# Attention outputs turned by the DMA crossbar instead of TensorE, and operand splits queued behind the division of the values, in a fused routing-attention and feed-forward kernel

## Chip, cores, metric

The kernel runs on one core of one Trainium2 chip. The metric is device microseconds of one execution; lower is better. A run is called slow when it lies over 1.5% above the fastest run of the same kernel, and slow runs are left out of all comparisons. Names: PE is TensorE, PEld its weight loads, DVE is VectorE, ACT is ScalarE, POOL is GpSimd, SP is SyncE. L378 is line 378 of the kernel.

## The reference

Clustered attention for 4 batches and 8 heads (768 rows of 64), then a feed-forward with h·cos(h) on all 3072 tokens:

```python
def _attn_ref(q, k, v, centroids):
    ...                                   # q_n, k_n, c_n: rows divided by their norms
    q_assign = np.argmax(np.einsum('bhsd,hcd->bhsc', q_n, c_n), axis=-1)
    k_assign = np.argmax(np.einsum('bhsd,hcd->bhsc', k_n, c_n), axis=-1)
    mask = q_assign[:, :, :, None] == k_assign[:, :, None, :]
    scores = np.where(mask, scale * np.matmul(q, k.transpose(0, 1, 3, 2)), -1e9)
    ...                                   # softmax
    return np.matmul(attn, v).astype(np.float32)

def _moe_ref(x, w_in, w_out):             # x: (3072, 512), d_ff 2048
    h = x @ w_in
    return ((h * np.cos(h)) @ w_out).astype(np.float32)
```

## The kernel before

Heads go in 16 pairs, four to a batch. A pair passes through these steps. `split` (DVE, half of it on POOL or ACT for some pairs) makes high and low fp16 parts of q and k. `tr`/`tr_out` or `tr_dma` turn them. `c_mm`/`c_post` find the clusters. `e_chunk` makes nine chunks of scores on PE (L332) with one exponential each on ACT (L339). `f_mm` multiplies by the values (L352) and `norm` divides (L362, L363). `g_tr` turns the result into `xt`, the feed-forward's input. After each fourth pair the feed-forward of that batch runs (`moe1`, L394 on PE, L401 on ACT, L402 on DVE; `moe2`, L416).

The turn of a pair's output, and what it waits for:

```python
    def norm(p, hh):
        av = f_of[p, hh]
        ...
        nc.vector.reciprocal(recip, av[:, :, D:DE])                         # L362
        dve_mark[0] = nc.vector.tensor_tensor(                              # L363
            out=av_of[p][:, :, hh, :], in0=av[:, :, 0:D],
            in1=recip.to_broadcast([P, NT, D]), op=ALU.mult).ins

    def g_tr(p):
        b, hp = divmod(p, HPB)                                              # HPB = 4
        ...
        if p >= NPE and hp < HPB - 1:                                       # NPE = 5
            nc.sync.dma_start_transpose(out=xt_of[b][:, hp]..., in_=st...)  # L373
            return
        trx = ps_one.tile([P, NT, P], FP16, name="one")
        for t in range(NT):                                                 # NT = 6
            nc.tensor.transpose(out=trx[:, t, :], in_=st[:, t], identity=ident)   # L378
        dve_mark[0] = nc.vector.tensor_copy(out=xt_of[b][:, hp, :], in_=trx...).ins  # L379
```

The first phase (pairs 0 to 4) is ordered by hand on all engines; its end, before the change:

```python
        for n_f, n_x in ((2, 0), (2, 1), (2, 1), (2, 1), (0, 0)):
            for _ in range(n_f):
                fl.pop(0)()            # value products of pair 3
            for _ in range(n_x):
                ex.pop(0)()            # g_tr of pairs 0, 1, 2
            if not n_x:
                sp.pop(0)()            # a split of pair 5
            chunk()                    # scores and exponential
        g_tr(s - 1)                    # pair 3
```

From pair 5 on ACT and POOL are ordered by hand, and a scheduler orders PE, DVE and SP from the order in which work is given. For pair s, r = s % 4, the work beside the nine chunks was given as

```python
            fill += trs("E", s)        # splits of a later pair: pair 9 in s = 8, pair 13 in s = 12
            if r != 1:
                fill += f_list(s - 1) + g_list(s - 1)   # values, division, turn of the pair before
```

The loads of q and k of pairs 9 and 13 are issued by POOL in the stretch before that of pairs 8 and 12, that is beside the scores of pairs 7 and 11, at chunks 3 (q) and 5 (k).

The softmax here doesn't subtract the row's maximum and nothing guards it: scores larger than these inputs give would overflow.

## Time and profile before

| | kernel before |
|---|---|
| time, median of 3 runs | 315.12 us (314.93 to 315.14) |
| span of the profiled run, granted clock | 313.0 us, 1.0 |
| PE busy / weight loads | 97% / 68% |
| ACT, DVE, POOL busy | 69%, 60%, 24% |
| turns of outputs on PE (L378), copies (L379) | 48 matmuls, 8 copies |
| turns of outputs by the crossbar (L373) | 8 |

Busy time of PE is modelled and matmuls overlap, so 97% says that PE is rarely without work, not that every instruction on it counts. What counts is which wait ends last in a stretch.

### The profile page before, as it was taken

Reading aid. Unit: us, or ns where it says so; the run is one execution under the profiler, and the core shown is the slowest. Engines: PE = TensorE matmul, PEld = TensorE weight load, DVE = VectorE, ACT = ScalarE, POOL = GpSimd, SP = SyncE. Lnnn points to the kernel's source line nnn. Section 1 sums busy time; section 2 is a strip of 40 time slices with the busy share of each in tenths; the row PEclk is TensorE's granted clock in tenths of the full one; section 3 lists DMA queues with packets and bytes.
Section 4 is the critical chain, followed back from the end, with each engine's and each line's share of the span. In section 5 each row is a group of like instructions: output and inputs, shape, how many; then the busy total and the mean of one; then the engine's idle time right before and its main releaser. Section 6 shows DMA issues by size and latency. Waiting matters only on the chain.

```text
span 313.0 us, 8197 instructions
## 1 busy us (share of the span) xinstructions
PE 303.1 (97%) x3459; PEld 213.8 (68%) x3459; DVE 189.0 (60%) x363; ACT 216.4 (69%) x235; POOL 74.7 (24%) x130
## 2 busy tenths in 40 slices
PE   7999999999999999899999999899999999999995
PEld 3668777888765766588775657497865657767754
DVE  5888897779966335369967144458965114455431
ACT  6688988955569999656659999756559996442220
POOL 2979945120130322210040233211020220000000
PEclk9999999999999999999999999999999999999999
DMA  6669999766596989837498997927576472000012
GB/s 213 203 141 185 218 113 146 168 153 153 78 241 131 154 128 150 163 104 172 70 229 127 177 114 180 162 86 179 87 165 99 80 74 61 12 24 36 34 57 80
DMA packets 87845, 40.25 MB, mean 129 GB/s; under 512 B 76352, under 2 KB 82752, under 8 KB 87808
## 3 DMA queue, kind: packets, MB, share of 16 engines
q1 hardware_dynamic: 57504, 24.19, 33.5%
q0 software_dynamic: 30016, 15.21, 33.1%
q8 instruction: 27, 0.44, 0.6%
q10 hardware_dynamic: 288, 0.33, 0.4%
q14 instruction: 10, 0.08, 0.1%
HBM read 27.30 MB, written 6.29 MB: 107 GB/s over the span
## 4 chain that ended last, share of the span: by engine, by line
PE 84%; DVE 7%; DMA 4%; ACT 1%; issue 1%; SPq 0%; POOL 0%; POOLq 0%; ACTq 0%; DVEq 0%
PE big L394 25%; PE one L416 24%; PE big L332 17%; PE one L352 8%; DMA qk_nat<-in_k_dram 4%; PE one L250 2%; PE one L247 2%; PE one L306 2%; DVE g L402 2%; DVE stg L200 2%; PE one L218 1%; DVE av_stage L363 1%; PE one L433 1%; DMA cn_raw<-in_centroids_dram 1%; PE one L378 1%
## 5 line engine op out<-in xcount | busy, mean ns | idle before, releaser
L339 ACT ACTIVATE e_ring<-big 128x1024 f16<-128x1024 f32 x144 | 138.4, 1030 | 16.1 <-PE big L332 14.8
L401 ACT ACTIVATE cos_t<-big,bias_pi 128x1024 f16<-128x1024 f32 x48 | 53.4, 1112 | 65.5 <-PE big L394 64.2
L416 PE MATMUL one<-w_out_sb,g 128*128 128x512 f16 x368 | 95.7, 379 | 0.0
L394 PE MATMUL big<-xt,w_in_sb 128*128 128x256 f16 x768 | 91.3, 273 | 1.0 <-DVE g L402 0.9
L332 PE MATMUL big<-qkT 128*128 128x512 f16 (+1 forms) x384 | 85.6, 325 | 0.5 <-ACT e_ring L339 0.4
L394 PEld LDWEIGHTS <-w_in_sb 128*128 128x128 f16 x768 | 74.0, 98 | 16.2 <-DVE g L402 1.7
L402 DVE TENSOR_TENSOR g<-big,cos_t 128x1024 f16<-128x1024 f32 x48 | 58.6, 1222 | 38.8 <-ACT cos_t L401 38.8
L416 PEld LDWEIGHTS <-g 128*128 128x128 f16 x368 | 35.0, 98 | 28.0
L332 PEld LDWEIGHTS <-qkT 128*128 128x128 f16 x384 | 32.8, 97 | 25.9 <-issue 4.3
L352 PEld LDWEIGHTS <-e_ring 128*128 128x128 f16 x1152 | 43.1, 97 | 7.0
L352 PE MATMUL one<-v_ext,e_ring 128*128 128x65 f16 x1152 | 45.2, 193 | 0.0
L421 DVE COPY o_sb<-one 128x512 f32<-128x512 f32 x23 | 15.8, 687 | 43.3 <-PE one L416 43.3
L200 DVE SCALAR_TENSOR_TENSOR stg<-qk_nat,stg 128x384 f16<-128x384 f32 x64 | 33.3, 553 | 0.2
L134 POOL DMA_DIRECT2D v_ext<-in_v_dram x32 | 26.5, 833 | 4.8 <-issue 2.4
L117 POOL COPY pace<-e_ring 1x1 f16<-1x1 f16 x30 | 5.7, 189 | 79.0 <-ACT e_ring L339 78.8
L117 POOL COPY pace<-g 1x1 f16<-1x1 f16 x13 | 2.3, 177 | 78.9 <-DVE g L402 70.1
L196 POOL TENSOR_SCALAR stg<-qk_nat 128x384 f16<-128x384 f32 x16 | 19.3, 1205 | 6.8 <-DMA qk_nat<-in_q_dram 5.7
L363 DVE TENSOR_TENSOR av_stage<-one,recip 128x384 f16<-128x384 f32 x32 | 17.7, 557 | 1.0
L362 DVE RECIPROCAL recip<-one 128x6 f32<-128x6 f32 x32 | 6.1, 192 | 19.4 <-PE one L352 19.4
L194 ACT ACTIVATE stg<-qk_nat 128x384 f16<-128x384 f32 x28 | 13.1, 512 | 1.9 <-DMA qk_nat<-in_q_dram 1.9
L318 DVE TENSOR_SCALAR qkT<-one 16x768 f16<-16x768 f16 (+1 forms) x20 | 10.9, 544 | 3.5 <-PE one L306 2.9
L258 DVE TENSOR_REDUCE csum<-one 128x192 f32<-128x384 f32 x22 | 11.2, 549 | 0.0
(57 smaller groups left out, 163.6 us busy)
## 6 DMA issues: line engine op xcount, KB each, us to landing
out_dram<-o_sb SPq DMA_DIRECT2D x23, 256.0 KB, 2.4
qk_nat<-in_q_dram POOLq DMA_DIRECT2D x10, 384.0 KB, 4.7
qk_nat<-in_k_dram POOLq DMA_DIRECT2D x10, 384.0 KB, 4.6
v_ext<-in_v_dram POOLq DMA_DIRECT2D x32, 96.0 KB, 4.0
w_in_sb<-in_moe_w_in_dram POOLq DMA_DIRECT2D x4, 512.0 KB, 6.3
w_out_sb<-in_moe_w_out_dram POOLq DMA_DIRECT2D x4, 512.0 KB, 6.1
qk_nat<-in_q_dram SPq DMA_DIRECT2D x5, 384.0 KB, 5.2
qk_nat<-in_k_dram SPq DMA_DIRECT2D x5, 384.0 KB, 5.9
```

The lines of the kernel that those rows point to most:

```text
L134: nc.gpsimd.dma_start(out=v_bufs[p % NV][:, hh, :, 0:D], in_=v[b, 2 * hp + hh].rearrange("(p t) d -> p t d", p=P))
L196: nc.gpsimd.tensor_scalar_mul(dst[:, :, 0, :], src, ASCALE)
L200: nc.vector.scalar_tensor_tensor(out=dst[:, :, 1, :], in0=src, scalar=ASCALE, in1=dst[:, :, 0, :], op0=ALU.mult, op1=ALU.subtract)
L332: mm = nc.tensor.matmul(ps[:, x:x + n], lhsT=qkT[p, 1, hh][:, jt * P:(jt + 1) * P], rhs=qkT[p, 0, hh][:, col:col + n], start=True, stop=True)
L339: nc.scalar.activation(out=e_flat[:, base + c * CW:base + (c + 1) * CW], in_=ps, func=AF.Exp, scale=1.0 / SUNIT)
L352: nc.tensor.matmul(av[:, i, :], lhsT=e_ring[:, r + j, i * P:(i + 1) * P], rhs=vx[:, j, 0:DE], start=(j == 0), stop=(j == NT - 1))
L363: dve_mark[0] = nc.vector.tensor_tensor(out=av_of[p][:, :, hh, :], in0=av[:, :, 0:D], in1=recip.to_broadcast([P, NT, D]), op=ALU.mult).ins
L394: mm = nc.tensor.matmul(ps[:, fi, :], lhsT=w_in_sb[:, ft, (f0 + fi) * P:(f0 + fi + 1) * P], rhs=xt_of[b][:, ft, cols], start=(ft == 0), st ...
L401: nc.scalar.activation(out=cos_t, in_=ps, func=AF.Sin, bias=bias_pi2, scale=1.0)
L402: dve_mark[0] = nc.vector.tensor_tensor(out=g[:, f0:f0 + FQ, :], in0=ps, in1=cos_t, op=ALU.mult).ins
L416: nc.tensor.matmul(ops, lhsT=g[:, f, i * P:(i + 1) * P], rhs=w_out_sb[:, f, :], start=(f == 0), stop=(f == NFPT - 1))
L421: nc.vector.tensor_copy(out=o_sb, in_=ops)
```

## The change

The intent is to take turns off PE and to stop a queued split from holding up a division that needs nothing from it. The whole diff:

```diff
@@ g_tr
-        if p >= NPE and hp < HPB - 1:
+        if hp < HPB - 1:
             nc.sync.dma_start_transpose(...)
             return
@@ end of the first phase
-        ex = [lambda p=p: g_tr(p) for p in range(s - 1)]
@@ in each unit of the first phase
             if f:
                 norm(*f)
+                if f[1]:
+                    g_tr(f[0])
@@ last five chunks
-        for n_f, n_x in ((2, 0), (2, 1), (2, 1), (2, 1), (0, 0)):
-            for _ in range(n_f):
-                fl.pop(0)()
-            for _ in range(n_x):
-                ex.pop(0)()
-            if not n_x:
+        for i in range(5):
+            if fl:
+                take(min(2, len(fl)))
+            if i in (0, 4):
                 sp.pop(0)()
             chunk()
@@ work beside the chunks of pair s
-            fill += trs("E", s)
+            if r:
+                fill += trs("E", s)
             if r != 1:
                 fill += f_list(s - 1) + g_list(s - 1)
+            if not r:
+                fill += trs("E", s)
```

## The prediction

> **What bounds the kernel now.** I read the page first, then the chain of waits, then the timeline of single engines in the stretches the diff touches. From the page, the busy line of each engine and the granted clock:
>
> ```profile
> PE 303.1 (97%) x3459; PEld 213.8 (68%) x3459; DVE 189.0 (60%) x363; ACT 216.4 (69%) x235; POOL 74.7 (24%) x130
> ...
> PEclk9999999999999999999999999999999999999999
> ```
>
> TensorE (PE) is covered for 97% of 313.0 us at full clock, so time is won in two ways only: PE instructions taken away where PE is really the pace, or PE gaps closed. A gap shows in the chain that ended last; these are its consecutive pieces near 116 us (start, length, what):
>
> ```profile
> 114.90 1.03 ACT e_ring L339
> 116.53 5.75 DMA qk_nat<-in_k_dram
> 122.73 0.93 DVE stg L200 x2
> 123.66 0.54 DVE stg L198 x2
> 124.20 0.94 DVE stg L200 x2
> 125.27 0.56 DVE av_stage L363
> 125.97 0.57 DVE av_stage L363
> 126.58 0.51 PE one L378 x6
> ```
>
> A load of keys, then the splits of pair 9 made from it on VectorE (DVE), then the division of the attention values of pair 7 (L363), then the turning of pair 7 on PE (L378), which stands in PE's fixed order before more work. Pair 7's values do not need the load: they are only queued behind the splits in DVE's order. The timeline of PE and DVE there (idle time and releaser in brackets):
>
> ```profile
> 122.90 0.71 PE L352 MATMUL one<-v_ext,e_ring 128*128 128x65 f16 x18
> 123.45 0.59 PE L332 MATMUL big<-qkT 128*128 128x512 f16 x2
> 124.24 0.59 PE L332 MATMUL big<-qkT 128*128 128x256 f16 x3 [0.19 <-ACT e_ring L339]
> 124.67 0.38 PE L416 MATMUL one<-w_out_sb,g 128*128 128x512 f16 x1
> 126.58 0.51 PE L378 MATMUL one<-ident,av_stage 128*128 128x128 f16 x6 [1.54 <-DVE av_stage L363]
> 126.93 0.81 PE L416 MATMUL one<-w_out_sb,g 128*128 128x512 f16 x3
> 127.58 0.60 PE L332 MATMUL big<-qkT 128*128 128x512 f16 x3
> ```
>
> The values of pair 7 are summed at about 123.5, PE has its last other work at 124.67, and stands 1.54 us for L378. The same happens 71 us later for pair 11 (196.40 to 197.84, idle 1.06 us). The waits view sums both: "PE one L378 <- DVE av_stage L363: 2.6, 2, 1.5".
>
> The other place is the end of the first phase, 51 to 60 us, where pairs 0 to 3 are turned on PE. From the timelines of ACT, PE and DVE:
>
> ```profile
> 50.97 9.04 ACT L339 ACTIVATE e_ring<-big 128x1024 f16<-128x1024 f32 x9 [0.56 <-PE big L332]
> 58.44 0.50 PE L378 MATMUL one<-ident,av_stage 128*128 128x128 f16 x6
> 59.14 0.49 PE L394 MATMUL big<-xt,w_in_sb 128*128 128x256 f16 x3
> 59.27 0.55 DVE L379 COPY xt<-one 128x768 f16<-128x768 f16 x1
> 59.89 0.27 PE L394 MATMUL big<-xt,w_in_sb 128*128 128x256 f16 x1
> ```
>
> Nine exponentials run on ScalarE (ACT) back to back, 1.004 us each, until 60.01: here ACT is the pace although PE reads as full. The feed-forward part (L394) starts at 59.14 and stops at its fourth matmul until the copy of pair 3's turned output (L379) ends at 59.82.
>
> **What the Trainium skill says.** (1) "VectorE: DVE Perf Modes", section The three transpose paths: a 128x128 turn takes 390 ns on TensorE into PSUM and 1309 ns through the DMA crossbar straight into SBUF, so the crossbar is slower alone but uses neither PE nor DVE. The trace: six turns in a row hold PE about 0.34 us (54.77 to the next group at 55.11), far under 6 x 390 because they are pipelined, plus a copy of 554 ns on DVE; the existing crossbar turns of outputs (L373, x8) hold the sync queue 1.23 us and land after 2.8/3.7/4.7 us (least, median, most). (2) "DMA: Bandwidth & Descriptors", section Issuing engines are not separate DMA queues: all DMAs share 16 engines and interleave. The DMA row of the page is at 9 tenths or near it in the slices before 60 us, so the new transfers meet the weight loads; the older crossbar turns in such company (ohT) took up to 6.7 us. (3) "Perfetto Trace Analysis", section Identifying the Most-Contended Engine: matmul busy time is no measure of how near PE is to its limit. The trace agrees: the 51 to 60 us stretch shows PE busy in full and is paced by ACT.
>
> **Part A, splits of pairs 9 and 13 behind the values.** Nothing is added or removed. In the stretches of pairs 8 and 12 the four splits (8 DVE instructions, about 3.7 us with 356 and 553 ns each) and their wait for the keys come after pair 7's (11's) division and copy. New order for pair 7: values complete at about 123.5, reciprocal 0.20, division 0.56, hence ready near 124.5. PE finishes what stands ahead of L378 at 124.67 + 0.22 (one matmul of 512 columns, by the 0.43 us that two take) = 124.9. So L378 goes at 124.9, then 0.34, then three L416 at 0.65 in sum, and L332 starts at 125.9 in place of 127.58: **1.7 us**. ACT can follow: its ten exponentials end at 126.08, and before it then stood 2.19 us for PE; the two buffers of "big" free at 125.08 and 126.08, before PE asks. For pair 11: 196.40 + 0.22 + 0.34 + 0.65 = 197.6 against 198.83: **1.2 us**. After that the splits run from about 125.5 to 129.3 and the crossbar turn of pair 9 goes out about 4 us later than at 125.16; it lands in 7.1 us (median of L234), about 136.5, and its first reader (L250, pair 9's centroid product) is at 142.56, less the 1.7. It stays hidden. Everything behind is PE-paced, so 2.9 us reach the end.
>
> **Part B, pairs 0 to 2 by the crossbar.** Removed from 51 to 60 us: 18 turns on PE (3 x 0.34 = 1.0 us) and three DVE copies (3 x 0.554 = 1.66 us). They lie in the ACT-paced stretch: the nine exponentials still end at 60.01 and PE waits more for their buffers (free at 54.99, 55.99, 57.0, 58.0), so the 1.0 us of PE time is not won. What is won: L378 of pair 3 still stands behind the last chunk at 58.0 + 0.43, but DVE has no copy of pair 2 at 57.95, so its split is done by about 58.9 and the copy of pair 3 starts when the turns are done, near 59.0, not 59.27. The feed-forward's fourth matmul comes **0.3 us** earlier; the next "big" buffer, free at 60.01, does not stop it. The added transfers are issued near 31, 41 and 51 us, after each pair's second division (30.43, 40.33, 50.11). The last has 59.14 - 50.7 = 8.4 us to land and takes 3 to 7. The queue they wait in also issues pair 5's loads, which go from 27.4 to about 32.3, but are first used at 54.71.
>
> **Part C, pair 4.** The condition also catches pair 4, which the title does not name: 6 turns and a copy leave PE and DVE near 67 us. There PE stops again at 68.98 for L402 (0.38 us idle), whose own path, from L394's end at 66.53 through L401 and L402 to 68.92, has no turn in it. The 0.34 us of PE only lengthen that gap unless the scheduler puts other work into it: **0 to 0.3 us**, I take 0.1.
>
> Sum: 1.7 + 1.2 + 0.3 + 0.1 = 3.3 us. I take off 0.2 for an order by the scheduler a little worse than assumed (PE, DVE and sync order after 60 us are its own): 3.1 us, hence 315.1 - 3.1 = **312.0 us**.
>
> **Rivals.** (1) Every removed PE instruction counts. For it: PE at 97%. 24 turns x 73 ns (row L378 of the groups: 48 matmuls, 4.0 us busy; in the weight-load row 2.9, 61 ns each) are 1.5 to 2.0 us; with part A's 2.9 this makes 310.2 to 310.7. Against it: ACT without a gap from 50.97 to 60.01. (2) The crossbar turn of pair 2 lands late, behind 512 KB weight loads and pair 4's values, and the feed-forward's first matmuls wait for it. For it: the DMA row is at its fullest at 52 to 58 us. Against it: 8.4 us of room, longest seen for this form 4.7 us. At 10 us it costs 1.5 us, so 313.5; a landing at 12 us brings 315. (3) The splits put off come back: pair 9's operand is late, or DVE, now in arrears at 129, is late with the output copies (L421) or the first L402. For it: splits now end only 2 us before the feed-forward starts. Against it: DVE is half idle there (0.48 mean over 112 to 144 us) and the first L402 in the kernel before starts about 2 us after its L394. It would give back 0.5 to 1.5 us: 312.5 to 313.5.
>
> **Range and chances.** Closing the two gaps is read straight from the trace; I hold it 85% sure to bring at least 2 us. Repeats of the kernel before lie within 0.2 us. Rival 1 pulls to 310.5, rivals 2 and 3 to 313.5: 310.8 to 313.6. Two per cent are 6.3 us, more than all idle PE time the change touches plus all PE time it removes (2.6 + 2.0 = 4.6 us), so faster by over 2% has 2%, slower 1%, within 2% 97%.
>
> **What the profile will show.** Part A right: the wait "PE one L378 <- DVE av_stage L363" gone or under 0.5 us; no wait on qk_nat in the chain near 116 and 188 us; the feed-forward of the second and third batch starts about 2.0 and 3.2 us earlier than at 131.03 and 202.29, counting part B. Part B right: ACT still nine in a row to about 60.0, and L394 resumed near 59.6, not 59.89; wrong if PE gains a full microsecond before 62 us, or if L394 waits on xt from a DMA. Part C right: L378 x24 and L379 x4, L373 x12, with a gap before L394 near 68.7 about as wide or wider than 0.38. The prediction fails if the time is over 313.6, most likely by rival 2 or 3, or under 310.8, by rival 1 or by a new order of the scheduler.

## The result, and the profile after

Ratios here are those for the fast runs of both kernels from the same rounds; they are not quite the ratios of the medians quoted.

| | before | after |
|---|---|---|
| runs | 315.12, 314.93, 315.14, 315.63 us | 311.01, 317.58, 311.77, 320.96 us |
| fast runs | 4 of 4 | 2 of 4 (the others at clock 0.995 and 0.989) |
| span of the profiled run | 313.0 us | 309.2 us |
| ratio of the fast runs | | 0.9879, 95% interval 0.9851 to 0.9907 |

The fast runs gained 3.8 us. Later, with six fast runs, the ratio was 0.9930 (below).

The page of the changed kernel, PE's line and the hardware queue's (packets, MB, share of the 16 DMA engines):

```profile
PE 301.0 (97%) x3435; PEld 212.2 (69%) x3435; DVE 187.6 (61%) x359; ACT 216.3 (70%) x235; POOL 74.9 (24%) x130
...
q1 hardware_dynamic: 60704, 24.98, 39.3%
```

24 matmuls and 4 DVE instructions are gone, which is four pairs, 0, 1, 2 and 4. The hardware queue went from 33.5% to 39.3% of the DMA engines' time.

PE near 124 us in the changed kernel (timeline, columns as in the prediction):

```profile
122.40 0.71 PE L352 MATMUL one<-v_ext,e_ring 128*128 128x65 f16 x18
123.74 0.59 PE L332 MATMUL big<-qkT 128*128 128x256 f16 x3 [0.19 <-ACT e_ring L339]
124.17 0.38 PE L416 MATMUL one<-w_out_sb,g 128*128 128x512 f16 x1
124.39 0.50 PE L378 MATMUL one<-ident,av_stage 128*128 128x128 f16 x6
124.72 0.81 PE L416 MATMUL one<-w_out_sb,g 128*128 128x512 f16 x3
```

L378 follows L416 after 0.22 us, with no idle time. The same holds for pair 11. In the waits view, L378's wait for av_stage is gone.

The end of the first phase in the changed kernel, from the timelines of ACT, PE and DVE:

```profile
51.23 8.45 ACT L339 ACTIVATE e_ring<-big 128x1024 f16<-128x1024 f32 x9 [0.56 <-PE big L332]
58.33 0.50 PE L378 MATMUL one<-ident,av_stage 128*128 128x128 f16 x6
58.82 0.49 PE L394 MATMUL big<-xt,w_in_sb 128*128 128x256 f16 x3
58.87 0.56 DVE L379 COPY xt<-one 128x768 f16<-128x768 f16 x1 [0.15 <-PE one L378]
59.48 1.58 PE L394 MATMUL big<-xt,w_in_sb 128*128 128x256 f16 x13
```

The nine exponentials, which the prediction held to be ACT's own pace, take 8.45 us, not 9.04.

To add up the change I read, from PE's timeline of each profile, the starts of five landmarks: the first score matmul (E0), the first L394 of each of the four feed-forward parts (F1 to F4), and the first matmul of the last output (L433). Differences in us:

| stretch | before | before, second profile | after | after, second profile |
|---|---|---|---|---|
| E0 to F1 | 48.88 | 48.88 | 48.30 | 48.30 |
| F1 to F2 (holds the stretch of pair 8) | 71.89 | 71.40 | 70.00 | 70.72 |
| F2 to F3 (pair 12) | 71.26 | 71.73 | 69.92 | 69.92 |
| F3 to F4 | 62.98 | 62.98 | 62.98 | 62.97 |
| F4 to last | 40.65 | 40.65 | 40.65 | 40.65 |
| sum | 295.66 | 295.64 | 291.85 | 292.56 |

In these four profiles stretches without a wait repeat to 0.01 us, so a stretch shows 0.1 us, which the times of runs do not. Between kernels with different edits they differ by 0.1 to 0.2 us also without a wait (F1 to F2 took 69.80 to 70.11), as the scheduler's order differs. The first profiles differ by 3.81 us: 0.58 before F1, 3.23 in the two stretches with the splits, nothing elsewhere between the landmarks. (Outside them, the start took 10.26 us before and 10.52 after, the end 7.11 and 6.86, which cancels.) Matching PE's instructions one by one, counted from E0, splits the 3.23 (to 0.02): 1.70 and 1.23 us arise at the two L378, 0.09 and 0.10 in the chunks just ahead of them, where the scheduler put the value products in another order, and 0.09 between the first and the fourth L394. The second profile of the changed kernel lost 0.72 us in F1 to F2, where PE stood 0.54 us at 119.66 us for a transfer of one-hot rows (qkT<-ohT).

### The profile page after: what moved, and what is told of

It reads as the page before. It is cut to its first block, busy times and chain, and to the rows that moved or that the text cites. A ratio compares the mean times of both kernels' runs of the same rounds, so it can differ in the third digit from the quotient of the medians.

```text
span 309.2 us, 8154 instructions
## 1 busy us (share of the span) xinstructions
PE 301.0 (97%) x3435; PEld 212.2 (69%) x3435; DVE 187.6 (61%) x359; ACT 216.3 (70%) x235; POOL 74.9 (24%) x130
## 3 DMA queue, kind: packets, MB, share of 16 engines
q1 hardware_dynamic: 60704, 24.98, 39.3%
## 4 chain that ended last, share of the span: by engine, by line
PE 87%; ACT 6%; DVE 4%; DMA 1%; issue 1%; ACTq 0%
PE one L416 25%; PE big L394 25%; PE big L332 18%; PE one L352 9%; ACT e_ring L339 5%; PE one L250 2%; PE one L247 2%; PE one L306 2%; DVE g L402 2%; PE one L218 2%; PE one L433 1%; DMA qk_nat<-in_q_dram 1%; ACT cos_t L401 1%; DVE qkT L318 1%; DVE av_stage L363 1%
## 5 line engine op out<-in xcount | busy, mean ns | idle before, releaser
L416 PE MATMUL one<-w_out_sb,g 128*128 128x512 f16 x368 | 95.7, 379 | 0.0
L394 PE MATMUL big<-xt,w_in_sb 128*128 128x256 f16 x768 | 91.4, 273 | 1.1 <-DVE g L402 1.0
L394 PEld LDWEIGHTS <-w_in_sb 128*128 128x128 f16 x768 | 73.9, 98 | 16.4 <-DVE g L402 2.4
L416 PEld LDWEIGHTS <-g 128*128 128x128 f16 x368 | 35.0, 97 | 28.1
L363 DVE TENSOR_TENSOR av_stage<-one,recip 128x384 f16<-128x384 f32 x32 | 17.8, 557 | 1.1
```

The lines of the kernel that those rows point to most:

```text
L363: dve_mark[0] = nc.vector.tensor_tensor(out=av_of[p][:, :, hh, :], in0=av[:, :, 0:D], in1=recip.to_broadcast([P, NT, D]), op=ALU.mult).ins
L394: mm = nc.tensor.matmul(ps[:, fi, :], lhsT=w_in_sb[:, ft, (f0 + fi) * P:(f0 + fi + 1) * P], rhs=xt_of[b][:, ft, cols], start=(ft == 0), st ...
L416: nc.tensor.matmul(ops, lhsT=g[:, f, i * P:(i + 1) * P], rhs=w_out_sb[:, f, :], start=(f == 0), stop=(f == NFPT - 1))
```

## The experiments

All were run beside the kernel before, on three chips. All gave correct results.

### The changed kernel again

> The changed kernel once more, to have more fast runs and to count slow ones (two of its first four were slow, none of four of the kernel before). Theory: fast runs near 311.4 us, 3.8 us under the kernel before. Rival on the slow state: closing the TensorE gaps makes the clock throttle, then about half of these runs are slow (316 us and more) and the kernel before stays without; if it is a matter of the chip or the moment, few or none are slow here, or the kernel before has some too.

Measured: 311.7 to 313.77 us, median 312.38 (6 runs, all fast); before 314.33 (11 runs); ratio 0.9930 (0.9901 to 0.9958). No run was slow, so the rival's forecast, about half of the runs, failed. Why two of the first four were slow stays open; the kernel before had three runs at clock 0.995 and 316 to 317 us. The gain was smaller than in the first rounds, and the times of the changed kernel spread over 2 us. What follows explains part of the spread.

### Only the new place of the splits

```diff
# to the kernel before: only the last hunk of the change
+            if not r:
+                fill += trs("E", s)
```

> Only the new place of the splits in the stretches of pairs 8 and 12, all turns on TensorE as before. Theory: the two gaps are closed by this alone, 1.80 and 1.33 us by the shift of the feed-forward's starts between the two traces, so about 312.1 us and the wait of L378 for av_stage nearly gone. Rival (the parts need one another, the crossbar turns free DVE and help close the gaps): under 2 us gained.

Measured: 312.72 us median (311.47 to 314.84), ratio 0.9938 (0.9900 to 0.9975). Both gaps before L378 are gone. F1 to F2 took 70.07 us, as in the changed kernel, so this part needs nothing from the others. F2 to F3 took 71.48 us and gained little, because a new wait stood at 142 us, just after F2 (PE and SP timelines of this run):

```profile
142.06 0.77 PE L250 MATMUL one<-cside,qkT 128*128 128x32 f16 x24 [1.39 <-DMA qkT<-stg]
```
```profile
128.78 5.82 SPq L234 DMA_TRANSPOSE qkT<-stg  x1
```

L250 is the centroid product of pair 9. Its operand is the crossbar turn (L234) that goes out after the splits. In the kernel before it went out at 125.16, here at 128.78. The landing times of L234 had least, median and most of 5.5/7.1/7.4 us before and 5.5/7.2/13.2 us here. Without the wait L250 would have started at 140.67, so a transfer with 4.7 us of room by its median became the one that ended last.

This wait (0.3 us or more) was in 5 of the 8 profiles with the new place: this one, and below those with pair 4 on PE (0.35 us), the turns put back (0.61 and 0.39), turn 1 twice (1.77) and turn 1 "later" (0.89). It was in none of the 6 with the old place. The landing itself is later in every profile: the turns of pairs 9 and 13 took 9.7 to 13.6 us in all 8 with the new place, 7.0 to 9.0 us in the 6 with the old one.

### Only the turns by the crossbar

```diff
# to the changed kernel: the last hunk undone
-            if r:
-                fill += trs("E", s)
+            fill += trs("E", s)
...
-            if not r:
-                fill += trs("E", s)
```

> Only the turns of pairs 0, 1, 2 and 4 by the crossbar, the old place of the splits. Theory now: 0.6 us gained, all before 61 us, because three of the nine exponentials at 51 to 60 us were paced by TensorE (starts 1.07 to 1.14 us apart, 0.90 in the changed kernel), so about 314.55 us. The prediction on record said 0.3 to 0.4 us. Rival of every removed instruction counting: 1.5 to 2 us.

Measured: 314.27 us median (312.05 to 315.4), ratio 0.9981 (0.9945 to 1.0017), no sure gain. E0 to F1 took 49.99 us in the profile, 1.11 more than in the kernel before, because of a stop of PE with no releaser (PE timeline of this run):

```profile
50.03 0.40 PE L247 MATMUL one<-cside,qkT 128*128 128x16 f16 x10
52.07 0.50 PE L247 MATMUL one<-cside,qkT 128*128 128x16 f16 x14 [1.64 <-issue]
...
126.76 0.51 PE L378 MATMUL one<-ident,av_stage 128*128 128x128 f16 x6 [0.33 <-DVE av_stage L363]
```

The stop falls within a group of 24 matmuls with the same operands. Less the stop, the stretch took 48.35 us, so 0.53 us of the expected 0.6 was gained and 1.64 lost. The gaps before L378 were here 0.33 and 0.37 us: this stretch came 1.4 us later, and the load of the keys, issued 1.39 us later (117.92 against 116.53), took 4.3 us to land, not 5.8, so that the splits went on at 122.21 against 122.31 us.

### What the stop is

Stops marked "issue" at 50 to 52 us were in 6 of the 10 profiles with early crossbar turns and in none of the 4 without. The DMA packets in the traces (read by start, duration and queue) show what goes with them. I list the start of the 16384-byte fetch on the instruction queue, the longest data packet between 43.5 and 49.5 us, and the stop:

```
profile          early turns   fetch starts   longest data packet    PE stop
before                no         45.52 us       0.97 us                 -
before, second        no         45.56          1.12                    -
only the splits       no         45.28          0.70                    -
early loads           no         45.44          1.07                    -
after                 yes        47.10          0.75                    -
after, second         yes        47.06          0.71                    -
copies put back       yes        47.00          0.88                    -
turn 1 twice          yes        46.70          1.50 (at 47.26)         -
candidate             yes        48.15          1.64 (at 44.90)       0.61 us
turns put back        yes        48.23          2.35 (at 44.67)       0.54
turn 1 "later"        yes        48.59          2.53 (at 44.51)       1.05
pair 4 on PE          yes        48.64          2.09 (at 44.86)       1.40
candidate, turn 1     yes        48.88          2.19 (at 45.09)       1.32
only the turns        yes        49.29          2.54 (at 44.95)       1.64
```

The page counts 27 fetches and 0.44 MB on this queue. The Trainium skill, "TensorE: Matmul & The Clock Gate", section Step-by-step: what each phase is for, speaks of "the 64-byte MATMUL instruction"; 0.44 MB by 64 bytes is about 6900, and PE has 3459 matmuls and as many weight loads, 6918. Between two fetches of the kernel before PE ran 252 instructions on average, and 16384 bytes are 256 times 64. In all six runs with a stop it comes after the same 735th matmul, in the middle of a group, and it ends 1.2 to 1.7 us after the fetch is complete. So I take this to be PE's own instruction stream, and the stop a wait for instructions, an inference. In the six stopped runs, packets that were under way at about 44.5 to 45.1 us, when the crossbar turn of pair 1 moves, took 1.6 to 2.5 us; the throughput fell to about 40 GB/s meanwhile (DMA view of the run with only the turns, 44 to 48 us in 40 slices, busy tenths and GB/s):

```profile
DMA  9997999999996999922222222226616000299999
GB/s 154 174 184 133 164 174 236 214 168 147 160 120 90 82 82 31 26 41 44 33 44 41 33 33 44 38 41 41 41 28 15 10 13 18 35 142 97 100 159 161
```

The fetch, which began at 45.28 to 45.56 us in the four profiles without these turns, began at 46.70 us or later in all ten with them, and PE stopped in those where it began at 48.15 us or later (no stop up to 47.10). So that the early turns put the fetch off is shown; by what means is not. Two experiments tried the cause further.

### The turn of pair 1 twice

```diff
                 if f[1]:
+                    if f[0] == 1:
+                        st = av_of[1].rearrange("p t h d -> p (t h d)")
+                        nc.sync.dma_start_transpose(out=spare..., in_=st)
                     g_tr(f[0])
```

> The changed kernel with the crossbar turn of pair 1 (issued at 41 us) done twice, the first time into a spare tile that nobody reads. Theory: the packets of this turn hold up the instruction fetch of TensorE (16384 bytes on the instruction queue), which began at 45.3 to 45.5 us in three profiles without the early turns and at 47.0 to 49.3 us in seven with them, and TensorE stood 0.5 to 1.6 us at 50 to 52 us, with no releaser, in the four where it began after 48.1. Twice the turn: the fetch begins at 49 us or later and TensorE stands 1.5 us or more. Rival (the stall is chance, unconnected with the turn): fetch and stall as in the changed kernel.

The expectation failed. The fetch began at 46.70 us and PE did not stop at 50 us, although the packets of the turn were twice as many. The long packets came here at 47.26, after the fetch had begun. So in this profile more turned data did not bring a stop, and the theory failed. What the six profiles with a stop share, and the others do not, is packets of over 1.6 us before the fetch; that these put it off is argued from the order in time alone, and what makes the packets long stays open. The clock was at 1.00 from 40 to 60 us in this profile, so the lower mean did not make the reading. This kernel had 314.73 and 317.3 us at clock 0.995 and 0.994, and waited 1.77 us for pair 9's operand; two runs give no more.

### The turn of pair 1 later

```diff
-                if f[1]:
+                if f[1] and f[0] != 1:
                     g_tr(f[0])
+                if f == (2, 0):
+                    g_tr(1)
```

> The changed kernel with the crossbar turn of pair 1 issued half a unit of scores later, after pair 2's first division at about 45.5 us instead of 41 us. Theory: the fetch is over before the turn's packets start, begins at 45.3 to 46 us, no stall at 50 us, and the times spread less than the changed kernel's 311.7 to 313.8 us, near its lower end. Rival: the turn delays the next fetch, or pair 2's turn behind it lands too late for the feed-forward at 58.8 us.

The edit did not move the transfer: it still went out at 41.06 us. In SP's timeline of this run it is the next issue after a load at 34.01 us, so its new place in the program had nothing else in SP's order to stand behind. So this is one more sample of the unmoved turn: fetch at 48.59, stop 1.05 us, 312.68 us median of the five fast runs (311.66 to 314.53; a sixth was slow, 317.21), ratio 0.9913 (0.9872 to 0.9955). Whether a really later turn would avoid the stop was not tried.

### The turns back on PE, without the copies

```diff
         for i in range(5):
             ...
+            if i in (1, 2, 3):
+                trx = ps_one.tile([P, NT, P], FP16, name="one")
+                for t in range(NT):
+                    nc.tensor.transpose(out=trx[:, t, :], in_=ident, identity=ident)
```

> The changed kernel with eighteen turns (of the identity, result unread) put back on TensorE at the old places at 53 to 57 us, without their copies on VectorE; output stays right. Theory: TensorE paced three of the nine exponentials there, so their starts go back to 1.07 to 1.14 us apart and the first feed-forward matmul comes 0.5 to 0.6 us later from the first score matmul than in the changed kernel (48.9 against 48.3 us). The reading on record (ScalarE is the pace, the turns are free): exponentials 0.90 us apart as in the changed kernel, no shift.

Starts of single exponentials, first in the kernel before, then in the changed one, then here (ACT timelines in narrow windows):

```profile
54.73 1.03 ACT L339 ACTIVATE e_ring<-big 128x1024 f16<-128x1024 f32 x1
55.80 1.02 ACT L339 ACTIVATE e_ring<-big 128x1024 f16<-128x1024 f32 x1
56.94 1.02 ACT L339 ACTIVATE e_ring<-big 128x1024 f16<-128x1024 f32 x1
58.07 1.02 ACT L339 ACTIVATE e_ring<-big 128x1024 f16<-128x1024 f32 x1
```
```profile
54.98 1.03 ACT L339 ACTIVATE e_ring<-big 128x1024 f16<-128x1024 f32 x1
55.88 1.05 ACT L339 ACTIVATE e_ring<-big 128x1024 f16<-128x1024 f32 x1
56.79 1.06 ACT L339 ACTIVATE e_ring<-big 128x1024 f16<-128x1024 f32 x1
```
```profile
55.33 1.04 ACT L339 ACTIVATE e_ring<-big 128x1024 f16<-128x1024 f32 x1
56.41 1.02 ACT L339 ACTIVATE e_ring<-big 128x1024 f16<-128x1024 f32 x1
57.55 1.02 ACT L339 ACTIVATE e_ring<-big 128x1024 f16<-128x1024 f32 x1
```

Before, the starts lie 1.07, 1.14 and 1.13 us apart; after, 0.90; with the turns back, 1.08 and 1.14. E0 to F1 was 49.47 us, less a stop of 0.54 us 48.93, as in the kernel before (48.88). So PE paced these chunks, and its 18 turns are the whole gain before F1. (F1 is the first L394; what comes after it is taken up in the next experiment.) Time: 312.55 us median (311.35 to 315.18), ratio 0.9934 (0.9880 to 0.9988), too wide to show 0.6 us.

### Three DVE instructions back, without the turns

```diff
+            if i in (1, 2, 3):
+                src = nat[NPE][:, 0, 0]
+                nc.vector.scalar_tensor_tensor(out=spare, in0=src, scalar=1.0, in1=src, ...)
```

> The changed kernel with three VectorE instructions of about 0.55 us (result unread) put back where the copies of pairs 0 to 2 stood, nothing on TensorE. Theory: no more than 0.1 us in the time of the first feed-forward matmul and exponentials still 0.90 us apart, since the gain was TensorE's. The working on record put 0.3 us on VectorE being free of the copy of pair 2: then the copy of pair 3 starts 0.3 us later and the fourth feed-forward matmul with it.

Exponentials 0.90 us apart, E0 to F1 48.30 us, both as in the changed kernel. But F1, the first L394, lies before the place where the copy of pair 3 can be felt: that is the fourth L394. The copy started 0.76 us after its turns, not 0.54, and the fourth L394 came 0.33 us later than in the changed kernel, as the working had it. Counted from E0, stops at 50 us taken off:

| | 18 turns on PE | DVE work of the copies | first L394 | fourth L394 | first L416 |
|---|---|---|---|---|---|
| before | yes | yes | 48.88 | 49.64 | 61.07 |
| turns put back | yes | no | 48.93 | 49.37 | 60.83 |
| copies put back | no | yes | 48.30 | 49.30 | 61.11 |
| after | no | no | 48.30 | 48.96 | 60.41 |

At the fourth L394 both count, and they nearly add up: 0.34 us for the turns alone, 0.27 for the copies alone, 0.68 together. By the first L416 this run had lost the whole 0.66 us of the changed kernel, and F1 to F2 took 70.71 us against 70.00. There the scheduler had also put a reciprocal (L363 here) before the first product with the cosine in DVE's order; DVE stood 2.18 us for it, until 63.23. How much of the loss is this order and how much the DVE time was not separated. Time: 313.18 us median of the three fast runs (311.37 to 313.69; a fourth was slow, 316.66), ratio 0.9931.

### Pair 4 on PE

```diff
-        if hp < HPB - 1:
+        if hp < HPB - 1 and p != NPE - 1:
```

> The changed kernel, pair 4 turned on TensorE again. Theory: nothing, within 0.1 us by the starts of the feed-forward's later groups; the gap before L394 near 68.5 us goes from 0.48 back to 0.38 us. Rival: pair 4's 0.34 us of TensorE come back in full.

F1 to F2 took 70.05 us against 70.00: nothing, as expected. The expected gap of 0.38 us before L394 did not come: none over 0.15 us is left, as the turn of pair 4 (from 68.70 us, 0.34 us) now stands in it. E0 to F1 had a stop of 1.40 us. Time 313.82 us median (312.99 to 316.18), ratio 0.9977 (0.9935 to 1.0019); the stop and a wait for the operand of pair 13 (0.35 us) are in it.

### Old place of the splits, earlier loads

```diff
# to the kernel before
-                    l_at("E", 4 * b + 3, 3, 4 * b + 5)
+                    l_at("E", 4 * b + 3, 0, 4 * b + 5)
```

> The kernel before with the old order, but the loads of pairs 9 and 13 issued three chunks (some 3 us) earlier. Theory: the gap before L378 came from the wait of the splits for the keys at the head of the DVE queue (2.50 and 2.07 us), so without this wait the splits end near 123.3 and L378 goes at about 125.1 in place of 126.58; second gap gone; gain 2.4 to 2.8 us, about 312.5 us. Rival: the 3.7 us of DVE work in the splits are the cause whatever they wait for, then the gap stays over half and the gain is under 1.5 us.

DVE and PE in this run (timelines):

```profile
119.79 0.62 DVE L198 TENSOR_SCALAR stg<-qk_nat 128x384 f16<-128x384 f32 x2
...
124.23 0.56 DVE L363 TENSOR_TENSOR av_stage<-one,recip 128x384 f16<-128x384 f32 x1
125.23 0.50 PE L378 MATMUL one<-ident,av_stage 128*128 128x128 f16 x6
```

The splits no longer wait, the division is done at 124.79, and L378 follows at 125.23 without idle time. F1 to F2 took 70.20 us, F2 to F3 70.11, sum 140.31 against 143.15 before and 139.92 after: 2.84 us gained with the order unchanged. So what held PE up was the wait for the keys at the head of the DVE queue, not the splits' own work. Time: 312.71 us median (312.21 to 313.16), ratio 0.9936 (0.9912 to 0.9961), the narrowest spread of the experiments with six runs. It has no early turns, and its pair 9's operand goes out early.

### Candidate: turns by the crossbar, old place, earlier loads

```diff
# to the kernel with only the turns by the crossbar
-                    l_at("E", 4 * b + 3, 3, 4 * b + 5)
+                    l_at("E", 4 * b + 3, 0, 4 * b + 5)
```

> A candidate: turns by the crossbar as in the change, but the splits in their old place with the loads of pairs 9 and 13 three chunks earlier. Theory: no gap before L378, and pair 9's operand is ready some 4 us sooner than in the changed kernel, so that its late crossbar transfer (1.39 us of waiting in the profile with the new order alone) can hold nothing up: as fast as the changed kernel or up to 0.5 us faster, some 312 us on a chip where that has 312.4, with a narrower spread. Rival: the earlier loads collide with other transfers and give it back.

Measured: 312.36 us median (311.68 to 313.61), ratio 0.9923 (0.9893 to 0.9953). No gaps, no wait for the operand, a stop of 0.61 us at 50 us.

### Candidate with the moved turn

```diff
# to the kernel with the turn of pair 1 "later"
-            if r:
-                fill += trs("E", s)
+            fill += trs("E", s)
...
-            if not r:
-                fill += trs("E", s)
...
-                    l_at("E", 4 * b + 3, 3, 4 * b + 5)
+                    l_at("E", 4 * b + 3, 0, 4 * b + 5)
```

> The same with the splits in their old place and the loads of pairs 9 and 13 three chunks earlier. Theory: no stall at 50 us, no gap before L378, no waiting for pair 9's operand; 311.5 us or less, the fastest so far. Rival: other transfers then collide and it stays at about 312.3 us like the kernel with early loads and unmoved turn.

Measured: 312.25 us median (311.09 to 313.54), ratio 0.9895 (0.9854 to 0.9935). As the turn did not move, it is the candidate above, with a stop of 1.32 us in its profile. Three of the eleven runs before that count as fast had a clock of 0.995 (316.2 to 317.1 us); without them the ratio of the means is 0.991 here and 0.993 for the turn "later". Neither candidate is shown to beat the change: the intervals overlap with 0.9879 and 0.9930.

### The kernel before again

> The kernel before once more for a second profile. Theory: fetch at 45.3 to 45.5 us and no stall at 50 us; two gaps before L378, whose sizes go with the landing of the keys and so differ from 1.54 and 1.06 us (with the old order and the crossbar turns they were 0.33 and 0.37 us).

The fetch and the absence of a stop were as expected (one run, 315.01 us, state unknown). The sizes of the gaps only changed places: 1.05 us at pair 7 and 1.54 us at pair 11, against 1.54 and 1.06.

## Why the prediction was right, and where not

- **Result.** 312.0 us was predicted, and the fast runs of the first rounds were 311.01 and 311.77. Most of the gain came from the place named first, the two gaps: 2.93 of 3.81 us between the first profiles. That the sum fits so well is in part luck: part B and the scheduler's order were taken too small (below), and the stop of PE and the late operand, which are not in the sum, took some of it back in other runs. Later, with six fast runs, the means are 2.2 us apart.
- **Part A.** Predicted 1.7 + 1.2 us; at the two L378 1.70 and 1.23 us were gained, so the mechanism and both sizes were right. The two stretches became 1.89 and 1.34 us shorter, 3.23 together (3.21 against the second profile of before); 0.19 of the rest came from the scheduler's order ahead of L378, for which the prediction had taken 0.2 off. The experiment with earlier loads showed the cause: with the wait for the keys taken away and the order left alone, L378 waits no more and 2.84 us are gained.
- **"It stays hidden"** is the step of part A that failed. The working let pair 9's transfer land in 7.1 us, the median before. Issued 3.3 to 3.6 us later it landed in 10.3 us in the changed kernel's first profile, with no wait, and in 13.2 us in the run with the new place alone, where PE stood 1.39 us. That other traffic delays it is likely but was not tested. The prediction named this as rival 3 with 0.5 to 1.5 us. In 5 of 8 profiles it happened.
- **Part B.** Predicted 0.3 us, measured 0.58 us before F1 and 0.68 at the fourth L394, the place that the prediction spoke of. The failed step is the reading "nine exponentials run back to back, 1.004 us each, here ACT is the pace". The merged line hid three slots of 1.07 to 1.14 us among slots of 0.90 to 1.01; 1.004 was only the mean. So the trace does not agree with what the prediction says under (3), that ACT paced the whole stretch. In those three slots PE was the pace, with a chunk, two value products and a turn. Putting the turns back on PE restored these slots; putting DVE work back did not. The DVE term of the sum, the fourth L394 0.3 us earlier, was right: 0.27 and 0.33 us in the two experiments. What was missing beside it is the 0.34 to 0.41 us of PE's turns, put at nothing.
- **Part B, what was left out.** No step looked at the instruction fetch. With the early transfers came stops of 0.54 to 1.64 us in 6 of 10 profiles, so this part is not shown to be worth anything in time: 0.9981 with it alone, interval over 1. Rival 2 looked for the harm in a late landing for the feed-forward, and no profile has such a wait. But its 8.4 us of room were nearly used: the turn of pair 2 took 5.7 to 9.2 us to land, not 3 to 7, and in the run with turn 1 "later" it landed 0.1 us before F1.
- **Part C.** Predicted 0.1 us, measured 0.05 at most. That the 0.34 us of PE only lengthen a gap is shown by the run with pair 4 on PE, where the turn filled it. The growth from 0.38 to 0.48 us fits the working but is no evidence by itself: with the turns put back the gap was 0.38 us too, with pair 4 on the crossbar.
- **Rival 1** fell: of the 1.5 to 2.0 us that it would have given, the removed PE work gave 0.58 us, where PE was the pace.

## What to carry to other kernels

When work queued behind a load blocks other work, move one behind the other, or issue the load earlier; the second leaves later users' transfers where they were. If you move the work back, take the landing time of what it sends at its longest, not at its median, beside the traffic that it will then meet. A merged run of instructions on one engine is not a pace: look at the starts one by one before calling the engine bound. When you split a gain between two engines, take a landmark that lies behind the effect of both. When you add DMA work to a stretch that is dense in short PE instructions, look for stops marked "issue".

## What the Trainium skill lacked or had wrong

- "DMA: Bandwidth & Descriptors", section Rules for kernel authors, says that a crossbar transpose next to ordinary DMAs "needs nothing". No run here gave a wrong result, so that holds for correctness. For time it lacks what was seen here: in 6 of 10 profiles with early turns, data packets took 1.6 to 2.5 us during one such transfer, while without these turns the longest at this place was 0.70 to 1.12 us (in the other four with early turns 0.71 to 1.50).
- "Runtime: NRT & Kernel Launch", section Instruction fetch mechanics, calls the cost of the fetch mostly hidden and names only a taken branch as what stalls it. By the inference above it was not hidden here, without a branch: a fetch that began at 48.15 us or later, in place of 45.5, went with a stop of PE of 0.54 to 1.64 us, marked "issue" without a releaser.
- "VectorE: DVE Perf Modes", section The three transpose paths, gives 390 ns for one turn on TensorE and does not say what one costs in a row. Six in a row held PE for 0.34 us in all, under 60 ns each.
